# Third chunk's x loads and VectorE's order written out in a block kernel's ramp, and one gate product moved by a slot

## The chip, the cores and the metric

The kernel runs on one core of a Trainium2 chip. A core has TensorE (PE, with its weight loads shown apart as PEld), VectorE (DVE), ScalarE (ACT), GpSimd (POOL) and SyncE (SP, which here only issues DMAs); each works through its own list of instructions in order and waits on semaphores of the others. The metric is the device time of one execution in microseconds, lower is better; the time before is the median of three runs.

## The reference

The input is x of 2048 rows by 640. A layer norm (without scale or shift) gives xn. The output is the sum of x, a windowed attention on xn and a gated MLP on xn:

```python
x = A_x
xn = _layernorm(x, axis=-1)
return x + _A_ref(xn, A_wqkv, A_wo) + _B_ref(xn, B_w_gate, B_w_up, B_w_down)
```

The attention has 32 heads of 20 columns; query i sees keys i-255 to i. The MLP is `(gelu(xn @ w_gate) * (xn @ w_up)) @ w_down` with 1728 hidden columns and the tanh form of gelu. Everything is float32.

## The kernel before, in words

Float32 precision is kept by splitting each operand into a high part (rounded to the matmul's type) and a low remainder and adding three products: high*high, low*high, high*low. So each product of 640 rows of weights is 15 matmuls (5 blocks of 128 rows, 3 products). Names ending in h and l, `xh` and `xl` above all, are the two parts.

**The ramp.** The 2048 rows of x are four chunks of 512, each four tiles `xi` of 128 rows. For a chunk, VectorE takes the statistics of each tile (`ln_stats`: two BN_STATS and one BN_AGGR, lines 149 to 151), works out the reciprocal root (`ln_sqrt`, `ln_rstd`, lines 156 to 165) and scales the tile (`ln_apply`, line 169). TensorE then transposes: `turn(k, ...)` (line 185) writes the k-th block of 128 columns of all four tiles into one PSUM tile `ps_t`; k runs over five. ScalarE copies each `ps_t` to `xh` (line 193), VectorE subtracts it to give `xl` (line 194). The letter handed to `turn` says which PSUM pool the tile comes from: "x" has two buffers, "m" four. In `ln_turn` before, the letters alternate x m x m x, so the fifth transpose takes a buffer that the first used.

Behind each chunk's transposes stand projections of it: `proj_v` (15 matmuls into `ps_v`) for four tiles of 128 rows, one chunk behind, and `proj_qk` (15 matmuls of 512 columns into `ps_d`) for two blocks of wqk, number 0 and number 5. `save_qk` stores a `ps_d`: `upper` on ScalarE (line 277, `pt<-ps_d`), `middle` on VectorE (line 273, `r<-ps_d,pt`; `r` has a single buffer), `lower` on ScalarE (line 255), `lowest` on GpSimd (line 259), then DMAs to `qd` or `kd`.

Chunk 0 is written out by hand in `first_chunk`, under a manual schedule in which every compute engine keeps the order of the code; its last lines take the statistics of chunk 1 (tiles 4 to 7), project v for tiles 0 and 1, and scale tiles 4 to 7. The rest of the ramp is code in an ordinary loop `for c in range(1, NC)`, whose order on each engine a scheduler sets when the program is built, and it merges with the end of the manual part too. The x tiles have eight buffers, so tiles 8 to 11 take those of 0 to 3, and their loads wait for the transposes of these; SyncE issues all DMAs of this stage in one order.

**The attention.** 32 units (8 groups of 4 heads, 4 chunks) run as a stream of 14 slots each (`NS = 14`), the order of every engine as written. In slots 0, 5 and 9 `pull_max(2, T)` emits two pairs of score products (`ps_m`, line 508) and VectorE's row maxima of them (line 518; two to a pair, in four PSUM buffers). In slot 0 a second `pull_max(2, T)` follows the product with v (`av_unit`, `ps_o`, line 616). Odd slots below 12 have two score products for the exponentials (`ps_e`, line 573) and ScalarE's exponentials (line 575). Between these, `pull_fill` feeds dense matmuls as filling: projections, and later the first gate and up products of the MLP (`gate_up_fill`).

A function that must come later is given to `defer(n, fn)`, which runs it n slots on; one wrapped in `late` runs at the slot's `flush()`, in slot 0 behind the first `pull_max` and the `av_unit`. A gate's chain is c1 (ScalarE: half of the product and its square, lines 670 and 671), c2 (VectorE: the product `he<-he,gs`, line 676), c3 (ScalarE: tanh, line 680; `lag()` slots after c2, one from slot 13, three from slot 0), c4 and c5 (VectorE, lines 684 and 691). There are 12 such gates.

**After the attention** come the rest of the MLP and the output product, both also written out; the change does not touch them.

Of the kernel before, what the change touches and what calls it, by code (L numbers as in the profile page):

```python
# [9 lines left out]
F32 = mybir.dt.float32  # L10
# [10 lines left out]
NC = S // C  # L21
# [9 lines left out]
NS = 14  # L31
# [36 lines left out]
def block_kernel(ctx, tc, x, wqk, wv, wgu, wdo, wdl, out):  # L68
# [73 lines left out]
    def ln_load(t, lp):  # L142
        xi = lp.tile([128, D], F32, name="xi", tag="xi", bufs=8)
        nc.sync.dma_start(xi, x[t * 128:(t + 1) * 128, :])
        return xi

    def ln_stats(xi, mv, lp):
        st = lp.tile([128, 2, 6], F32, name="st", tag="st", bufs=4)
        nc.vector.bn_stats(st[:, 0, :], xi[:, 0:320])  # L149
        nc.vector.bn_stats(st[:, 1, :], xi[:, 320:640])  # L150
        nc.vector.bn_aggr(mv, st)
# [16 lines left out]
    def ln_apply(xi, mv, rs):  # L168
        nc.vector.tensor_scalar(xi, xi, mv[:, 0:1], rs, op0=OP.subtract, op1=OP.mult)

    def ln_scale(xs, lp):
        n = len(xs)
        mv = lp.tile([128, n, 2], F32, name="mv4", tag="mv4", bufs=2)
        for i, xi in enumerate(xs):
            ln_stats(xi, mv[:, i, :], lp)
        rs = ln_rstd(*ln_sqrt(mv, n, lp), n, lp)
        for i, xi in enumerate(xs):
            ln_apply(xi, mv[:, i, :], rs[:, i:i + 1])

    def turn(k, xs, where):  # L180
        n = len(xs)
        pool, tag = {"x": (psx, "ex"), "m": (psm, "mx"), "o": (psm, "mx")}[where]
        ps = pool.tile([128, n * 128], F32, name="ps_t", tag=tag)
        for i in range(n):
            nc.tensor.transpose(ps[:, i * 128:(i + 1) * 128], xs[i][:, k * 128:(k + 1) * 128], ident)  # L185
        return ps

    def ln_turn(t0, xs):
        n = len(xs)
        cs = slice(t0 * 128, (t0 + n) * 128)  # L190
        for k in range(KT):
            ps = turn(k, xs, "xm"[k % 2])
            nc.scalar.activation(xh[:, k, cs], ps, AF.Copy)
            nc.vector.tensor_tensor(out=xl[:, k, cs], in0=ps, in1=xh[:, k, cs].bitcast(F32), op=OP.subtract)  # L194

# [23 lines left out]
    def defer(n, fn, *a):  # L219
        if now[0] is None:  # L220
            fn(*a)
        else:
            at(now[0] + n, fn, *a)
# [121 lines left out]
    def first_chunk(xs, wr0, wr5, prep, v0, lp):  # L345
# [26 lines left out]
        with tc.manual_schedule(engines=MANUAL | {mybir.EngineType.Pool}):  # L372
# [27 lines left out]
            for k in range(KT):  # L400
                low(k, ta[k], halves[0])
            tb = [turn(k, xs[2:4], "oxmxm"[k]) for k in range(KT)]
            for k in range(KT):
                high(k, tb[k], halves[1])
            for k in range(KT):
# [20 lines left out]
            for j in range(4):  # L426
                ln_apply(xs[4 + j], mv[:, j, :], rs[:, j:j + 1])
            save_qk(0, 0, dn[0])
            save_qk(5, 0, dn[1])
        return w0, w5, v0  # L430

    v0 = []
    with tc.tile_pool(name="lp", bufs=1, side="right") as lp:
        xs = [ln_load(t, lp) for t in range(2)]
        wr0 = load_qk(0)
        xs += [ln_load(t, lp) for t in (2, 3)]
        wr5 = load_qk(5)
        warm = lp.tile([128, 256], BF, name="warm")[:, 0:128]
        nc.vector.memset(warm, 0.0)
        ps = psd.tile([128, C], F32, name="ps_u", tag="dn")  # L440
        for i, n in enumerate(WARM):
            if i:
                nc.tensor.transpose(ps[:, 0:128], xs[1][:, 0:128], ident)
            for _ in range(n):
                nc.tensor.matmul(ps[:, 0:128], warm, warm, start=True, stop=True)
        prep = load_v(0, v0, lp, v_tiles())
        next(prep)
        xs += [ln_load(t, lp) for t in range(4, 8)]
        w0, w5, v0 = first_chunk(xs, wr0, wr5, prep, v0, lp)
        ones = lp.tile([4, 2 * C], BF, name="ones")  # L450
        nc.gpsimd.memset(ones, 0.0)
        nc.gpsimd.memset(ones[0:2], 1.0)
        for i in range(NK):
            for j in (0, 2):
                nc.sync.dma_start(ks[i][SR:64, j:j + 2].rearrange("p j t -> p (j t)"), ones)
        for c in range(1, NC):
            if c > 1:
                ln_scale(xs[4 * c:4 * c + 4], lp)
            ln_turn(4 * c, xs[4 * c:4 * c + 4])
            if c + 1 < NC:  # L460
                xs += [ln_load(t, lp) for t in range(4 * c + 4, 4 * c + 8)]
            if c == 1:
                for i in range(NQ):
                    for j in (0, 2):
                        nc.sync.dma_start(qs[i][SR + 2:64, j:j + 2].rearrange("p j t -> p (j t)"), ones[2:4])
            if c == 2:
                raws1 = [load_qk(1), load_qk(6)]
            if c < NC - 1:
                run(*[proj_v(v0, 4 * c - 4 + i, None if i % 2 else (psm, "mx")) for i in range(0 if c > 1 else 2, 4)])
                run(proj_qk(0, w0, c), proj_qk(5, w5, c))  # L470
# [191 lines left out]
    def gate_up_fill(f, ws, c):  # L662
# [4 lines left out]
        def c1():  # L667
            gs = st["g"] = hp.tile([128, C], F32, name="gs", tag="gs")
            t = st["t"] = hp.tile([128, C], F32, name="he", tag="he", bufs=2)
            nc.scalar.activation(gs, pss[0], AF.Copy, scale=0.5)  # L670
            nc.scalar.activation(t, pss[0], AF.Square, scale=math.sqrt(0.044715))
            defer(1, late, c2)

        def c2():
            gs, t = st["g"], st["t"]
# [853 lines left out]
```

## Time and profile before

| what | value |
|---|---|
| median of 3 runs | 1043.57 us (1043.51 to 1044.68) |
| the profiled execution | 1044.74 us, its span 1043.0 us |
| granted TensorE clock | 0.999 |
| PE busy | 1031.9 us, 99% of the span |
| DVE, ACT, POOL busy | 741.3, 528.0, 384.5 us (71%, 51%, 37%) |
| DMA moved | 158.74 MB, mean 152 GB/s |

A row of the timeline reads: start, duration (of the whole merged group), engine, line, operation, output<-input, shape, count, and in brackets the idle time of the engine just before it and what ended it. A start and the next row's start on one engine give the time that a group takes; durations of pipelined matmuls overlap. A row of the waits reads: who waited, for whom, total us, times, longest us.

### The profile page before, as it was taken

What the parts mean: (1) busy time and instruction counts of PE and PEld (TensorE: products, weight loads), DVE (VectorE), ACT (ScalarE), POOL (GpSimd) and SP (SyncE); (2) the same over time, 40 slices, a digit from 0 to 9 for tenths busy, and PEclk for the clock granted to TensorE, in tenths of its full rate; (3) what the DMA queues carried; (4) which work ended last, traced back from release to release, by engine and by line L of the source; (5) the groups of instructions that cost most, each with busy time, mean ns of one, the idle gap of its engine ahead of it and who ended that gap; (6) DMA issues with size and microseconds to landing.
All of it is one profiled execution on the core that took longest, in us unless ns stands there. A gap on an engine that the chain in (4) does not pass through costs nothing.

```text
span 1043.0 us, 25570 instructions
## 1 busy us (share of the span) xinstructions
PE 1031.9 (99%) x9396; PEld 833.9 (80%) x9396; DVE 741.3 (71%) x2018; ACT 528.0 (51%) x1120; POOL 384.5 (37%) x623
## 2 busy tenths in 40 slices
PE   8999999999999999999999999999999999999998
PEld 7987666666777666666678888888888999999998
DVE  7745666677656676677736777775556889888887
ACT  4534766767666666666675222223324554333332
POOL 5122778888765787667471111101110000000000
PEclk9999999999999999999999999999999999999999
DMA  6542356555533354343325576763117874433333
GB/s 224 181 143 70 98 168 184 160 172 160 179 94 100 116 162 147 97 130 120 97 75 192 187 244 210 247 242 120 73 62 264 255 245 135 139 127 114 124 122 107
DMA packets 102151, 158.74 MB, mean 152 GB/s; under 512 B 14173, under 2 KB 55261, under 8 KB 102025
## 3 DMA queue, kind: packets, MB, share of 16 engines
q1 hardware_dynamic: 99640, 150.94, 45.2%
q10 hardware_dynamic: 2384, 6.16, 1.9%
q8 instruction: 74, 1.21, 0.5%
q14 instruction: 53, 0.43, 0.1%
HBM read 101.78 MB, written 54.92 MB: 150 GB/s over the span
## 4 chain that ended last, share of the span: by engine, by line
PE 93%; DVE 4%; ACT 1%; DMA 1%; issue 1%; POOL 0%; DVEq 0%; SPq 0%; ACTq 0%
PE ps_g L973 23%; PE ps L1245 23%; PE ps_d L108 20%; PE ps_e L573 8%; PE ps_v L108 6%; PE ps_o L616 5%; PE ps_m L508 5%; DVE junk L518 2%; PE ps_g L108 1%; DMA xi<-x 1%; PE ps_d L356 1%; DVE xl L194 0%; PE ps_t L185 0%; DVE st L149 0%; DVE st L150 0%
## 5 line engine op out<-in xcount | busy, mean ns | idle before, releaser
L518 DVE CUSTOM_DVE_ANT_0 junk<-ps_m,mask 128x320 bf16<-128x320 f32 (+2 forms) x512 | 243.0, 475 | 129.1 <-PE ps_m L508 71.2
L575 ACT ACTIVATE P<-ps_e 128x512 f32<-128x512 f32 (+2 forms) x384 | 198.7, 572 | 68.6 <-PE ps_e L573 68.1
L1245 PE MATMUL ps<-wb,at 128*128 128x320 f32 x999 | 155.9, 309 | 0.0
L1245 PEld LDWEIGHTS ps<-wb,at 128*128 128x128 f32 x999 | 148.9, 188 | 0.2
L588 POOL TENSOR_SCALAR_AFFINE_SELECT P<-P 128x256 f32<-128x256 f32 (+1 forms) x192 | 94.1, 492 | 73.4 <-ACT P L575 70.1
L573 PE MATMUL ps_e<-qs,ks 124*128 124x128 bf16 (+2 forms) x704 | 118.3, 278 | 0.1
L108 PE MATMUL ps_d<-xl,wqh 128*128 128x512 f32 x310 | 98.5, 422 | 0.0
L108 PE MATMUL ps_d<-xh,wqh 128*128 128x512 f32 x310 | 98.2, 421 | 0.0
L108 PE MATMUL ps_d<-xh,wql 128*128 128x512 f32 x310 | 97.6, 419 | 0.0
L101 POOL TENSOR_TENSOR wql<-wr,wqh 128x640 fp32r<-128x640 f32 x12 | 19.2, 1604 | 195.7 <-PE ps_g L973 171.2
L1245 PE MATMUL ps<-wt,at 128*128 128x320 f32 x552 | 88.9, 309 | 0.0
L573 PEld LDWEIGHTS <-ks 124*128 124x128 bf16 x704 | 49.5, 98 | 48.9 <-issue 33.4
L1245 PEld LDWEIGHTS ps<-wt,at 128*128 128x128 f32 x552 | 82.9, 188 | 0.1
L591 POOL TENSOR_SCALAR_AFFINE_SELECT P<-P 128x512 f32<-128x512 f32 (+1 forms) x144 | 76.4, 539 | 16.3 <-ACT P L575 16.3
L1199 ACT ACTIVATE at<-ss 128x512 fp32r<-128x512 f32 x59 | 37.3, 632 | 84.1 <-DVE ss L1078 84.1
L616 PE MATMUL ps_o<-P,v 64*32 64x320 f32 (+4 forms) x2816 | 74.2, 347 | 0.0
L259 POOL TENSOR_TENSOR pt<-r,pt 128x512 bf16<-128x512 f32 x40 | 46.6, 1165 | 65.4 <-ACT pt L255 64.9
L616 PEld LDWEIGHTS ps_o<-P,v 64*32 64x32 f32 x2816 | 50.9, 106 | 21.5 <-issue 0.9
L508 PE MATMUL ps_m<-ks,qs 60*64 60x320 bf16 (+3 forms) x1472 | 64.5, 260 | 2.8 <-DVE mx L518 1.5
L1002 ACT ACTIVATE hr<-hr 128x512 f32<-128x512 f32 x20 | 12.6, 632 | 102.0 <-DVE hr L976 102.0
L108 PEld LDWEIGHTS ps_d<-xh,wql 128*128 128x128 f32 x310 | 56.0, 189 | 10.1 <-issue 0.9
L108 PEld LDWEIGHTS ps_d<-xh,wqh 128*128 128x128 f32 x310 | 56.0, 189 | 9.7 <-issue 1.6
(197 smaller groups left out, 1982.3 us busy)
## 6 DMA issues: line engine op xcount, KB each, us to landing
hd<-he SPq DMA_DIRECT2D x50, 256.0 KB
hr<-hd SPq DMA_DIRECT2D x48, 256.0 KB
wr<-wgu SPq DMA_DIRECT2D x27, 320.0 KB
qs<-qd SPq DMA_DIRECT2D x64, 120.0 KB
ks<-kd SPq DMA_DIRECT2D x64, 120.0 KB
xi<-x SPq DMA_DIRECT2D x16, 320.0 KB
qs<-qd SPq DMA_DIRECT2D x64, 80.0 KB
ks<-kd SPq DMA_DIRECT2D x64, 80.0 KB
```

The costliest lines, as they stand in the source:

```text
L108: nc.tensor.matmul(ps, a(k), b(k), start=n == 0, stop=n == 3 * nk - 1)
L259: nc.gpsimd.tensor_tensor(out=pt[:, l, :], in0=r, in1=pt[:, 1, :], op=OP.subtract)
L508: nc.tensor.matmul(ps[64 * h:64 * h + 64, col:col + w], q[rows, j, q0:q0 + 64], ks_, start=True, stop=True, tile_position=(64 * r, 64 * h))
L518: nc.vector.tensor_tensor_reduce(out=junk[:, 0:n], in0=ps[:, 320 - n:320], in1=mask[:, 320 - n:320], scale=1.0, scalar=NEG, op0=OP.add, op ...
L573: nc.tensor.matmul(ps[:, col:col + n], k[0:QROWS, j, kc:kc + 128], q[0:QROWS, j, q0:q0 + n], start=True, stop=True)
L575: nc.scalar.activation(pt[:, j, lo:hi], ps[:, lo:hi], AF.Exp, scale=SCALE)
L588: nc.gpsimd.affine_select(out=a, in_=a, pattern=[[0, n], [1, 128]], compare_op=OP.is_ge, fill=0.0, base=0, channel_multiplier=-1)
L591: nc.gpsimd.affine_select(out=a, in_=a, pattern=[[0, n], [-1, 128]], compare_op=OP.is_ge, fill=0.0, base=-1, channel_multiplier=1)
L616: nc.tensor.matmul(os[r][32 * j:32 * j + 32, qa:qb], v[rows, w0_:w0_ + 32], pt[rows, j, col + qa - q0:col + qb - q0], start=r not in begun ...
L973: nc.tensor.matmul(ps, i, j, start=first and n == 0, stop=n == len(work) - 1, skip_group_check=True)
L1199: nc.scalar.activation(hi[:, 3:7], s, AF.Copy)
L1245: nc.tensor.matmul(ps[bank][:, 0:HD], *work[bank][j], start=bank not in begun, stop=final[p, bank] == n and j == len(work[bank]) - 1, skip ...
```

## The change

Four edits in the ramp and one in the attention:

1. The loads of tiles 8 to 11 move from the loop's first round into `first_chunk`, right behind the transposes of tiles 2 and 3 in the code. The loop no longer loads in its first round.
2. The statistics of tiles 8 and 9 are taken inside the manual part, between `save_qk(0, 0, ...)` and its end; their tile `mv` is handed out and `ln_scale` for chunk 2 begins at tile 10.
3. `save_qk(5, 0, ...)` stands outside the manual part.
4. The transposes of chunks 1 and 2 take PSUM buffers "xmxmm" in place of "xmxmx"; chunk 3 keeps "xmxmx".
5. A gate whose c1 falls in slot 12 defers c2 by two slots, to slot 0 of the next unit, and not by one to slot 13.

```diff
-    def ln_scale(xs, lp):
+    def ln_scale(xs, lp, mv=None, begun=0):
         n = len(xs)
-        mv = lp.tile([128, n, 2], F32, name="mv4", tag="mv4", bufs=2)
-        for i, xi in enumerate(xs):
-            ln_stats(xi, mv[:, i, :], lp)
+        mv = mv or lp.tile([128, n, 2], F32, name="mv4", tag="mv4", bufs=2)
+        for i in range(begun, n):
+            ln_stats(xs[i], mv[:, i, :], lp)
...
-    def ln_turn(t0, xs):
+    def ln_turn(t0, xs, where="xmxmx"):
...
-            ps = turn(k, xs, "xm"[k % 2])
+            ps = turn(k, xs, where[k])
...
             tb = [turn(k, xs[2:4], "oxmxm"[k]) for k in range(KT)]
+            xs += [ln_load(t, lp) for t in range(8, 12)]
...
             save_qk(0, 0, dn[0])
-            save_qk(5, 0, dn[1])
-        return w0, w5, v0
+            mv = lp.tile([128, 4, 2], F32, name="mv4", tag="mv4", bufs=2)
+            for j in range(2):
+                ln_stats(xs[8 + j], mv[:, j, :], lp)
+        save_qk(5, 0, dn[1])
+        return w0, w5, v0, mv
...
             if c > 1:
-                ln_scale(xs[4 * c:4 * c + 4], lp)
-            ln_turn(4 * c, xs[4 * c:4 * c + 4])
-            if c + 1 < NC:
+                ln_scale(xs[4 * c:4 * c + 4], lp, *((mv, 2) if c == 2 else ()))
+            ln_turn(4 * c, xs[4 * c:4 * c + 4], "xmxmx" if c == NC - 1 else "xmxmm")
+            if 1 < c < NC - 1:
                 xs += [ln_load(t, lp) for t in range(4 * c + 4, 4 * c + 8)]
...
-            defer(1, late, c2)
+            defer(2 if now[0] is not None and now[0] % NS == NS - 2 else 1, late, c2)
```

What this does to the engines' orders is seen in four places. The first is VectorE between the statistics of tile 7 and the scaling of chunk 1. Before (`mv_470` is chunk 1's statistics, `mv_705` chunk 2's):

```order
L156 TENSOR_TENSOR ve<-mv_470,one 128x4
L162 RECIPROCAL rs<-sq 128x4
L151 BN_AGGR mv_705<-st 128x2
L149 BN_STATS st<-xi 128x6
L163 TENSOR_TENSOR ve<-ve,rs 128x4
L150 BN_STATS st<-xi 128x6
L164 SCALAR_TENSOR_TENSOR ve<-ve,rs 128x4
L149 BN_STATS st<-xi 128x6
L165 SCALAR_TENSOR_TENSOR rs<-ve,rs 128x4
L151 BN_AGGR mv_705<-st 128x2
L150 BN_STATS st<-xi 128x6
L169 TENSOR_SCALAR xi<-xi,mv_470,rs 128x640 x4
```

The same place on VectorE after the change (`mv_478` is chunk 1's statistics, `mv_556` chunk 2's):

```order
L156 TENSOR_TENSOR ve<-mv_478,one 128x4
L162 RECIPROCAL rs<-sq 128x4
L163 TENSOR_TENSOR ve<-ve,rs 128x4
L164 SCALAR_TENSOR_TENSOR ve<-ve,rs 128x4
L165 SCALAR_TENSOR_TENSOR rs<-ve,rs 128x4
L169 TENSOR_SCALAR xi<-xi,mv_478,rs 128x640 x4
L273 TENSOR_TENSOR r<-ps_d,pt 128x512
L149 BN_STATS st<-xi 128x6
L150 BN_STATS st<-xi 128x6
L194 TENSOR_TENSOR xl_81<-ps_t,xh_77 128x512
```

The statistics of tiles 8 to 10, which stood in front of chunk 1's scaling, stand behind it.

The second place is VectorE around the scaling of chunk 2. Before (`mv_910` is chunk 3's statistics):

```order
L156 TENSOR_TENSOR ve<-mv_705,one 128x4
L151 BN_AGGR mv_910<-st 128x2
L162 RECIPROCAL rs<-sq 128x4
L163 TENSOR_TENSOR ve<-ve,rs 128x4
L164 SCALAR_TENSOR_TENSOR ve<-ve,rs 128x4
L165 SCALAR_TENSOR_TENSOR rs<-ve,rs 128x4
L169 TENSOR_SCALAR xi<-xi,mv_705,rs 128x640 x4
L273 TENSOR_TENSOR r<-ps_d,pt 128x512
```

And after; the two L273 are `middle` for wqk blocks 0 and 5 of chunk 1:

```order
L163 TENSOR_TENSOR ve<-ve,rs 128x4
L150 BN_STATS st<-xi 128x6
L273 TENSOR_TENSOR r<-ps_d,pt 128x512
L164 SCALAR_TENSOR_TENSOR ve<-ve,rs 128x4
L151 BN_AGGR mv_910<-st 128x2
L149 BN_STATS st<-xi 128x6
L165 SCALAR_TENSOR_TENSOR rs<-ve,rs 128x4
L150 BN_STATS st<-xi 128x6
L169 TENSOR_SCALAR xi<-xi,mv_556,rs 128x640 x3
L273 TENSOR_TENSOR r<-ps_d,pt 128x512
L169 TENSOR_SCALAR xi<-xi,mv_556,rs 128x640
```

Statistics of tiles 13 and 14 and both `middle` steps have come in front of the scaling of chunk 2's last tile; before, the four scalings stood together and in front of both.

The third place is TensorE at the transposes of chunk 2. Before:

```order
L108 MATMUL ps_d<-xl_81,wqh 128x512 x5
L185 MATMUL ps_t<-ident,xi 128x128 x16
L108 MATMUL ps_v<-wvh,xh_77 128x320 x3
L185 MATMUL ps_t<-ident,xi 128x128 x4
L108 MATMUL ps_v<-wvh,xh_77 128x320 x2
```

And after:

```order
L108 MATMUL ps_d<-xl_81,wqh 128x512 x5
L185 MATMUL ps_t<-ident,xi 128x128 x15
L108 MATMUL ps_v<-wvh,xh_77 128x320 x2
L185 MATMUL ps_t<-ident,xi 128x128 x5
L108 MATMUL ps_v<-wvh,xh_77 128x320 x3
```

The 16 went block by block over all four tiles, and the 4 were the fifth block; the 15 are the blocks of tiles 8, 9 and 10, tile by tile, and the 5 are tile 11. In chunk 1 the 16 and 4 become 20 together.

The fourth place is VectorE at the first of the three gates that the fifth edit moves, where a unit begins; the ISA rows are maxima and the reads of their result. Before:

```order
L518 ISA mx 128x1
L676 SCALAR_TENSOR_TENSOR he<-he,gs 128x512
L518 ISA junk,mx<-ps_m,mask 128x320
L518 ISA mx 128x1
L518 ISA junk,mx<-ps_m,mask 128x320
```

And after (lines below the edits in the ramp carry numbers four higher):

```order
L522 ISA junk,mx<-ps_m,mask 128x320
L522 ISA mx 128x1
L522 ISA junk,mx<-ps_m,mask 128x320
L522 ISA mx 128x1
L680 SCALAR_TENSOR_TENSOR he<-he,gs 128x512
L522 ISA junk,mx<-ps_m,mask 128x320
```

The product has moved behind the four maxima of slot 0's first pull. On ScalarE the gate's tanh moves with it, from in front of the two copies of `ps_o` to behind the next two exponentials. SyncE issues the loads of tiles 8 and 9 right behind those of tiles 4 to 7, tiles 10 and 11 behind three of the eight small loads of ones that `ks` needs, tile 13 between the stores of `qd` and `kd`, and the second of the two loads of `wr` behind tile 15.

More of the change, by code (lines that the diff above doesn't have):

```diff
@@ L448, in block_kernel @@
         xs += [ln_load(t, lp) for t in range(4, 8)]
[L449 removed]
+        w0, w5, v0, mv = first_chunk(xs, wr0, wr5, prep, v0, lp)
         ones = lp.tile([4, 2 * C], BF, name="ones")
```

## The prediction

> **What bounds the kernel.** I read the page first, then TensorE's waits, then the timeline where they fall.
>
> ```profile
> span 1043.0 us, 25570 instructions
> PE 1031.9 (99%) x9396; PEld 833.9 (80%) x9396; DVE 741.3 (71%) x2018; ACT 528.0 (51%) x1120; POOL 384.5 (37%) x623
> ```
>
> TensorE is the bound: whatever it stands still less, the kernel should be shorter by. It has only these waits for other engines in the whole span:
>
> ```profile
> PE ps_t L185 <- DVE xi L169: 2.5, 4, 1.1
> PE ps_m L508 <- DVE mx L518: 1.5, 5, 0.4
> PE ps_t L185 <- DVE xl L194: 0.8, 2, 0.6
> ```
>
> All name VectorE: transposes that wait for scaled x tiles, score products that wait for maxima to free PSUM, and a fifth transpose that waits for `xl` to free its buffer. The change works at all three. TensorE in the ramp (gap before the group in brackets):
>
> ```profile
> 23.48 0.90 PE L108 MATMUL ps_v<-wvl,xh 128*128 128x320 f32 x5
> ...
> 25.42 2.46 PE L185 MATMUL ps_t<-ident,xi 128*128 128x128 f32 x16 [1.05 <-DVE xi L169]
> ...
> 30.36 0.90 PE L108 MATMUL ps_v<-wvh,xh 128*128 128x320 f32 x5
> ...
> 32.56 1.32 PE L108 MATMUL ps_d<-xh,wqh 128*128 128x512 f32 x5
> ...
> 39.39 1.91 PE L185 MATMUL ps_t<-ident,xi 128*128 128x128 f32 x16
> 41.05 0.69 PE L108 MATMUL ps_v<-wvh,xh 128*128 128x320 f32 x3
> 42.38 0.66 PE L185 MATMUL ps_t<-ident,xi 128*128 128x128 f32 x4 [0.65 <-DVE xl L194]
> 42.80 0.54 PE L108 MATMUL ps_v<-wvh,xh 128*128 128x320 f32 x2
> ```
>
> The group at 25.42 is chunk 1's transposes, late by 1.05 us; that at 39.39 is chunk 2's, not late, but its fifth block waits 0.65 at 42.38. VectorE over the same stretch shows why:
>
> ```profile
> 19.36 0.48 DVE L150 BATCH_NORM_STATS2 st<-xi 128x6 f32<-128x320 f32 x1
> 20.54 0.49 DVE L149 BATCH_NORM_STATS2 st<-xi 128x6 f32<-128x320 f32 x1 [0.70 <-DMA xi<-x]
> ...
> 23.73 0.49 DVE L149 BATCH_NORM_STATS2 st<-xi 128x6 f32<-128x320 f32 x1 [0.99 <-DMA xi<-x]
> ...
> 27.23 0.67 DVE L273 TENSOR_TENSOR r<-ps_d,pt 128x512 f32<-128x512 f32 x1
> ...
> 30.75 1.96 DVE L194 TENSOR_TENSOR xl<-ps_t,xh 128x512 fp32r<-128x512 f32 x3
> 32.62 0.48 DVE L150 BATCH_NORM_STATS2 st<-xi 128x6 f32<-128x320 f32 x1
> ...
> 34.87 2.18 DVE L169 TENSOR_SCALAR xi<-xi,mv,rs 128x640 f32<-128x640 f32 x4
> ```
>
> Chunk 1's statistics end with the row at 19.36. Then VectorE waits twice for loads of tiles 8 and 10, which chunk 1 has no need of, with chunk 1's scaling queued behind.
>
> **Chunk 1's transposes (edits 1 to 4).** The statistics of tiles 8 to 10 leave the way. By the rows at 32.62 and 34.87, 2.25 us lie between a late statistics row and the scaling, and that stretch holds another tile's statistics as well. So chunk 1's scaling starts by 19.36 + 2.25 = 21.6 and, at 2.18 for four, ends by 23.8. TensorE is ready when v of tile 1 is issued: a group of five v matmuls takes (32.56 - 30.36)/3 = 0.73, so at 23.48 + 0.73 = 24.21. It no longer waits. Sixteen transposes without a wait took 41.05 - 39.39 = 1.66, 0.104 each; twenty take 2.08, to 26.29. All five fit without a wait for `xl`, since "m" has a buffer free for the fifth. Two v tiles (2 x 2.20) reach 30.69, two wqk blocks (39.39 - 32.56 = 6.83) reach 37.52. TensorE comes to chunk 2's transposes 39.39 - 37.52 = 1.87 us earlier.
>
> **Chunk 2's transposes: what is late next.** VectorE's work has not gone, it stands later. Its order from the end of chunk 1 on, started by ScalarE's copy:
>
> ```profile
> 24.89 0.63 ACT L277 ACTIVATE pt<-ps_d 128x512 bf16<-128x512 f32 x1
> 27.26 1.09 ACT L193 ACTIVATE xh<-ps_t 128x512 fp32r<-128x512 f32 x2 [1.74 <-PE ps_t L185]
> ...
> 39.63 0.60 ACT L277 ACTIVATE pt<-ps_d 128x512 bf16<-128x512 f32 x1 [1.31 <-POOL pt L259]
> ```
>
> ```profile
> 28.94 1.17 POOL L259 TENSOR_TENSOR pt<-r,pt 128x512 bf16<-128x512 f32 x1 [9.28 <-ACT pt L255]
> ```
>
> `pt` is ready at 25.52. I price a statistics row at 0.40 (two in a row before), a `r` at 0.67, an `xl` at (32.62 - 30.75)/3 = 0.62, an aggregation between others at 0.12. From 25.6: r 26.3, tile 8 27.1, one xl and its aggregation 27.8, tile 9 28.6, r and aggregation 29.4, four xl 31.9. ScalarE's copies (0.55 each) and GpSimd's step (1.17) run ahead of these and do not hold them. Then: tile 10 and half of tile 11 1.3 (33.2), the stretch like 32.62 to 34.87 2.25 (35.45), and in between, new here, the four rows of tiles 13 and 14, r and an aggregation, 1.6 + 0.67 + 0.12 = 2.4. The first scaling starts at 37.8, or at 37.3 if the small steps hide between the larger ones as they may. TensorE is ready at 37.52, and needs a scaled tile some 0.75 after a scaling starts. So these transposes now wait for VectorE.
>
> There is more. GpSimd's step of 1.17 us for the `r` in this stretch starts 0.67 + 0.63 + 0.15 = 1.45 after that r, the scaling about 1.7 after it (r, aggregation, two statistics rows and the small steps). They overlap, GpSimd 0.25 ahead. Once in the trace a scaling met a GpSimd operation:
>
> ```profile
> 10.95 0.94 POOL L452 MEMSET ones<- 2x1024 bf16 x1
> ...
> 11.36 0.88 DVE L169 TENSOR_SCALAR xi<-xi,mv,rs 128x640 f32<-128x640 f32 x1
> ```
>
> The scaling took 0.88 in place of 0.61, and ended 0.35 behind the memset's end at 11.89. I take it that it was held till then. The Trainium skill ("SBUF — State Buffer", section "Who interferes with whom") says that VectorE's tensor_scalar in a 2-port mode and GpSimd share one port pair, locked for a whole instruction by whichever starts first; the row agrees. With the hold, GpSimd ends at 38.2 to 38.7, the first scaling at 38.55 to 39.05, the third (0.545 each) at 39.65 to 40.15. Then the second r stands in front of the fourth scaling; its `pt` is there (TensorE 37.52 + 0.24 + 0.60 = 38.4, by the rows at 39.39 and 39.63). The fourth ends 0.61 + 0.55 later, at 40.8 to 41.3, and tile 11's five transposes are over 0.14 + 0.52 later: 41.45 to 41.95. Before, the same work (20 transposes, two v matmuls) was over at 42.80 - 0.15 = 42.65. The ramp gains 0.7 to 1.2; without the hold 1.3 to 1.85; with VectorE no limit at all, 2.75. I take 1.1, near the upper end of the case with the hold, as small steps hid well before.
>
> Hidden and priced at nothing: the earlier x loads wait on SyncE for transposes of tiles 0 to 3, but the loads of ones behind them wait for GpSimd's memset to 11.89 anyway, and ones, like `wr`, is used only after the ramp. If that cover went, SyncE's later loads would slip (rival 4). Behind chunk 2's transposes stand four v tiles, 8.8 us, over which VectorE finishes `xl`. Chunk 3's order is as before.
>
> **The gate's product (edit 5).** Three of twelve are moved. The first, on TensorE and VectorE, and the other two on TensorE:
>
> ```profile
> 428.85 0.72 DVE L676 SCALAR_TENSOR_TENSOR he<-he,gs 128x512 f32<-128x512 f32 x1 [1.27 <-ACT he L671]
> 429.50 0.48 DVE L518 CUSTOM_DVE_ANT_0 junk<-ps_m,mask 128x320 bf16<-128x320 f32 x1
> ```
>
> ```profile
> 431.25 0.46 PE L508 MATMUL ps_m<-ks,qs 60*64 60x320 bf16 x5
> ...
> 432.23 0.73 PE L108 MATMUL ps_d<-xh,wql 128*128 128x512 f32 x2
> ...
> 444.98 0.33 PE L508 MATMUL ps_m<-ks,qs 60*64 60x320 bf16 x4
> ...
> 446.44 0.73 PE L108 MATMUL ps_d<-xh,wql 128*128 128x512 f32 x2
> ...
> 460.40 0.46 PE L508 MATMUL ps_m<-ks,qs 60*64 60x320 bf16 x5
> ...
> 461.35 0.73 PE L108 MATMUL ps_d<-xh,wql 128*128 128x512 f32 x2
> ```
>
> The product waits for ScalarE and takes 0.65 of VectorE ahead of the first maximum. The second pull's eight score products then need 0.98, 1.46 and 0.95 us. Another unit has its product already behind the four maxima:
>
> ```profile
> 402.76 0.91 DVE L676 SCALAR_TENSOR_TENSOR he<-he,gs 128x512 f32<-128x512 f32 x1
> ...
> 402.81 0.47 PE L508 MATMUL ps_m<-ks,qs 60*64 60x320 bf16 x8
> 403.21 0.73 PE L108 MATMUL ps_d<-xh,wqh 128*128 128x512 f32 x2
> ```
>
> There the eight need 0.40, and VectorE's product starts at 402.76 without holding anybody. So the first and third lose 0.58 and 0.55. The second loses 1.06, but gets back no more than the 0.65 by which its maxima come earlier; I take 0.6. The sum is 1.75 by starts; the waits named by the profile give less, since part of the gap lies under the modelled ends. The tanh, now behind two exponentials, finds ScalarE idle; VectorE's second four maxima start as before.
>
> **Sum.** 1.1 + 1.75 = 2.85 us of the profiled span of 1043.0 (its run took 1044.74, 1.2 over the median). From the median 1043.57 that leaves 1040.7, 0.27% less. About 0.2%, 2.1 us, is what a measurement of this kernel can tell from no change.
>
> **Rivals.**
> 1. No hold by GpSimd: GpSimd ends first or the scaling starts first, by a margin of 0.25 us. Ramp 1.3 to 2.0, together 3.05 to 3.75, 1039.8 to 1040.5. For it: a lead so small. Against: the row at 11.36.
> 2. VectorE is later still in chunk 2, from one wait of 0.7 more. Ramp 0.4, together 2.1, 1041.4. For it: VectorE, not TensorE, sets this stretch, so each delay counts in full.
> 3. The moved product only hands its wait to the second four maxima. Ramp alone, 1042.5. Against: the unit at 402.76.
> 4. Slower: the loads of tiles 13 and 14 come too late. Their statistics stand in VectorE's order ahead of chunk 2's scaling.
>
> ```profile
> 33.68 1.40 SPq L144 DMA_DIRECT2D xi<-x  x3
> ```
>
> ```profile
> 38.27 0.49 DVE L149 BATCH_NORM_STATS2 st<-xi 128x6 f32<-128x320 f32 x1 [0.61 <-DMA xi<-x]
> ```
>
> Before, tile 13 took 4.6 us from issue to statistics. After, tile 14 is issued behind the stores of the second r, at about 32.4 (29.3 + 0.6 + 1.3 for ScalarE and GpSimd, 1.2 for stores), so it is there by 37.0. It is needed at 36.3 to 36.9, and up to 0.7 of lateness vanishes under GpSimd's hold. Beyond, each us costs one; for 0.2% slower, 1045.7, it would have to land 5 us later, at about 42.
> 5. The ramp's gain and the gates' are given back later, no change. Against: 99% busy, and the orders behind are the same.
>
> **Chances.** Forecast 0.42; rival 1 0.20; rival 2 0.18, half of it past 0.2%; rival 3 0.10; rival 4 0.03; rival 5 0.07. Faster by over 0.2%: 0.42 + 0.20 + 0.09 = 0.71; within: 0.26; slower: 0.03. The range takes in the forecast and rivals 1 and 2 (0.80) with 0.2 to 0.5 us of scatter: 1039.6 to 1042.0.
>
> **What would show it.** Right: no wait at chunk 1's 20 transposes, which start near 24.2; chunk 2's start near 38.5 and wait for scaled tiles, with one scaling longer than 0.61 beside GpSimd; eight score products in 0.40 at the first and third moved gate. Wrong: a wait of VectorE for x loads between 30 and 37, transposes of tile 11 over after 42.6, or a wait for maxima still there at the gates.

## The result and the profile after

The changed kernel takes 1042.3 us, the median of 22 executions (1041.73 to 1044.85). The kernel before, run beside it, takes 1044.71 us (22 executions, 1043.51 to 1046.68). The ratio is 0.9975, with a 95% interval of 0.9969 to 0.9982: 1.9 to 3.2 us less, 2.6 in the middle. The profiled execution took 1043.06 us, its span is 1041.3 us, 1.7 less than the span of the profile before.

TensorE's waits for other engines in the changed kernel (total us, times, longest us):

```profile
PE ps_t L185 <- DVE xi L169: 1.2, 3, 0.8
PE ps_u L449 <- DVE warm L443: 1.2, 1, 1.2
PE ps_m L512 <- DMA qs<-qd: 1.1, 2, 0.6
PE ps_m L512 <- DVE mx L522: 0.6, 2, 0.4
PE ps_t L185 <- DVE xl L194: 0.2, 1, 0.2
PE ps_m L512 <- DVE xl L194: 0.2, 1, 0.2
```

The three waits that the change works at went from 2.5, 1.5 and 0.8 us to 1.2, 0.6 and 0.2. The third row is new: score products wait for a load of `qs`. The second and the last row stand in the profile before as well, with the same 1.2 and 0.2 us.

**The ramp.** The timeline of the changed kernel on TensorE, VectorE and GpSimd:

```profile
24.18 2.34 PE L185 MATMUL ps_t<-ident,xi 128*128 128x128 f32 x20
...
38.56 2.03 PE L185 MATMUL ps_t<-ident,xi 128*128 128x128 f32 x15 [0.82 <-DVE xi L169]
...
40.73 0.77 PE L185 MATMUL ps_t<-ident,xi 128*128 128x128 f32 x5
...
49.84 1.32 PE L108 MATMUL ps_d<-xh,wqh 128*128 128x512 f32 x5
```

```profile
21.29 2.18 DVE L169 TENSOR_SCALAR xi<-xi,mv,rs 128x640 f32<-128x640 f32 x4
...
37.19 2.37 DVE L169 TENSOR_SCALAR xi<-xi,mv,rs 128x640 f32<-128x640 f32 x3
39.48 0.68 DVE L273 TENSOR_TENSOR r<-ps_d,pt 128x512 f32<-128x512 f32 x1
40.08 0.60 DVE L169 TENSOR_SCALAR xi<-xi,mv,rs 128x640 f32<-128x640 f32 x1
```

```profile
37.00 1.16 POOL L259 TENSOR_TENSOR pt<-r,pt 128x512 bf16<-128x512 f32 x1 [5.54 <-ACT pt L255]
```

And the row in the profile before that answers to TensorE's last:

```profile
51.24 1.32 PE L108 MATMUL ps_d<-xh,wqh 128*128 128x512 f32 x5
```

Chunk 1's twenty transposes come without a wait. Chunk 2's wait 0.82 us for scaled tiles, and three scalings take 2.37 us beside GpSimd's step. At the projection of chunk 2, TensorE is 51.24 - 49.84 = 1.40 us ahead. I call this difference, of one matmul's start in the profile before and of the same matmul's start in another profile, the lead.

**The gates.** Score products on TensorE after, around the first moved gate, and the same two groups before:

```profile
428.75 0.47 PE L512 MATMUL ps_m<-ks,qs 60*64 60x256 bf16 x16
431.53 0.47 PE L512 MATMUL ps_m<-ks,qs 60*64 60x320 bf16 x8
435.36 0.47 PE L512 MATMUL ps_m<-ks,qs 60*64 60x256 bf16 x16
```

```profile
428.47 0.47 PE L508 MATMUL ps_m<-ks,qs 60*64 60x256 bf16 x16
...
431.25 0.46 PE L508 MATMUL ps_m<-ks,qs 60*64 60x320 bf16 x5
431.97 0.33 PE L508 MATMUL ps_m<-ks,qs 60*64 60x320 bf16 x3 [0.26 <-DVE mx L518]
...
435.67 0.47 PE L508 MATMUL ps_m<-ks,qs 60*64 60x256 bf16 x16
```

From one group of sixteen to the next it took 435.67 - 428.47 = 7.20 us and takes 6.61: 0.59 gained, and the eight in between stand together, where five and three stood apart before. At the second and third gate the lead grows by 0.60 and 0.57 us, over all three by 1.76.

**What is given back.** The lead is not 1.40 us when the gates come but -0.28 (428.47 against 428.75). Most of it goes here. `qs` holds a unit's queries, loaded back from `qd` by six DMAs, and `wr` raw weights; SPq rows are SyncE's issues. TensorE and SyncE after:

```profile
166.32 0.27 PE L512 MATMUL ps_m<-ks,qs 60*64 60x256 bf16 x1 [0.60 <-DMA qs<-qd]
167.10 0.47 PE L512 MATMUL ps_m<-ks,qs 60*64 60x256 bf16 x15 [0.51 <-DMA qs<-qd]
```

```profile
157.91 0.86 SPq L234 DMA_DIRECT2D wr<-wqk  x2
158.88 1.32 SPq L268 DMA_DIRECT2D qd<-pt  x2
160.30 4.74 SPq L487 DMA_DIRECT2D qs<-qd  x6
```

Before, the same sixteen score products start at 166.70, and the view names no wait:

```profile
166.70 0.65 PE L508 MATMUL ps_m<-ks,qs 60*64 60x256 bf16 x16
```

The landing records of the trace, where each of these DMAs lands in sixteen parts or eleven, show why TensorE waited (start of the issue, when the last but one of the parts was there, when the last):

```
load      issued   last but one   last part
wr  (1st) 157.91   160.78         160.79
wr  (2nd) 158.35   162.28         164.71
qs  (2nd) 160.84   163.88         166.19
qs  (5th) 162.36   165.28         166.96
qs  (6th) 164.72   167.23         167.55
```

Of the second `wr` load one part in sixteen landed 2.43 us behind the others, and in each of the seven DMAs behind it, too, one part came 1.7 to 2.4 us late. Two of the seven are the second and the fifth load of `qs`, and it is their semaphores that TensorE waits for here: it goes on at 166.32, 0.13 us behind the last part of the second, and at 167.10, 0.14 behind that of the fifth. The Trainium skill ("DMA: Bandwidth & Descriptors", section "Why a DMA increments its semaphore by 16 and not by 1") says that only the full count means that all data has landed; the rows agree, one late part holds the whole DMA.

SyncE was held as well. It issues a DMA only when the one eight before it is there, and the sixth load of `qs` is eighth behind that `wr` load, so it was not issued before 164.72. But these score products do not wait for the sixth load: they went on at 167.10, and it was there at 167.55.

### The profile page after: what moved, and what is told of

It reads as the page before. It is cut to its first block, busy times and chain, and to the rows that moved or that the text cites. A ratio compares the mean times of both kernels' runs of the same rounds, so it can differ in the third digit from the quotient of the medians.

```text
span 1041.3 us, 25568 instructions
## 1 busy us (share of the span) xinstructions
PE 1031.8 (99%) x9396; PEld 834.4 (80%) x9396; DVE 740.3 (71%) x2018; ACT 527.9 (51%) x1120; POOL 384.5 (37%) x623
## 4 chain that ended last, share of the span: by engine, by line
PE 92%; DVE 5%; DMA 1%; issue 1%; ACT 1%; SPq 0%; DVEq 0%; ACTq 0%
PE ps_g L977 24%; PE ps L1249 23%; PE ps_d L108 19%; PE ps_e L577 8%; PE ps_v L108 6%; PE ps_o L620 5%; PE ps_m L512 5%; DVE junk L522 2%; PE ps_g L108 1%; PE ps_d L356 1%; DVE xi L169 0%; DMA qs<-qd 0%; PE ps_t L185 0%; DVE st L150 0%; DVE xl L194 0%
## 5 line engine op out<-in xcount | busy, mean ns | idle before, releaser
L1203 ACT ACTIVATE at<-ss 128x512 fp32r<-128x512 f32 x59 | 37.3, 632 | 83.3 <-DVE ss L1082 83.3
```

Source lines behind the costliest of these rows:

```text
L1203: nc.scalar.activation(hi[:, 3:7], s, AF.Copy)
```

## The experiments

Two theories stood at the beginning: A, the ramp's gain is given back since TensorE runs into loads that do not come earlier with it; B, that was chance in one execution. From the fifth run on a third, D: the profile before showed a ramp that was worse than most. Where a lead is given, it is against the first profile before. "At 57 us" is behind the ramp, "at 300 us" behind the stretch with the late loads and ahead of the gates.

### The changed kernel again, and its parts alone

No edit in the first; in the second the gate's edit taken back; in the third it alone, on the kernel before:

```diff
-            defer(2 if now[0] is not None and now[0] % NS == NS - 2 else 1, late, c2)
+            defer(1, late, c2)
```

> The changed kernel once more. Its first profiled execution gained 1.40 us in the ramp and 1.68 us at the three gates, but lost 1.25 us at 166 us, where score products waited 0.60 and 0.51 us for a load of qs, and 0.36 us around 155 us. Theory A (the loads of this stretch set the pace: the ramp's gain brings TensorE to 166 us before the load that it needs, in most executions): a wait for qs at 166 us again, of 0.2 to 1.3 us, and a span of 1040.2 to 1041.4 us. Theory B (the wait was chance in that one execution): no wait for qs, TensorE 1.0 us or more ahead of the kernel before at 170 us, and a span near 1040.0 us.

> The four edits in the ramp without the gate's. Both theories: TensorE 1.40 us ahead of the kernel before at 57 to 151 us, and the waits for maxima at the three gates as before (1.68 us by starts). Theory A: the loads near 160 us take 0.3 to 1.3 us of it back, so that 0.1 to 1.1 us is left, 0.5 us in the median. Theory B: 1.4 us is left at the end. Rival C (the ramp's edits are worth nothing and all comes from the gates): no change.

> The kernel before with the gate's edit alone. The edit lies far behind the stretch at 150 to 170 us, so by both theories its gain of 1.68 us (0.50, 0.63 and 0.55 at the three gates) stays to the end: 1.5 to 1.8 us less than before, and the ramp as before. Rival C (the gates give back what they gain in the dense stage behind them): less than 0.5 us.

The changed kernel again: 1042.71 us, ratio 0.9982 (0.9973 to 0.9991). No wait is named at 166 us this time, but one at 238 us:

```profile
237.05 0.21 PE L512 MATMUL ps_m<-ks,qs 60*64 60x64 bf16 x1
238.23 0.36 PE L512 MATMUL ps_m<-ks,qs 60*64 60x64 bf16 x11 [0.97 <-DVE r L273]
```

VectorE's `r`, which the row names, was over at 237.89. The fifth `qs` load of that unit, issued at 232.91, had all of its parts but one by 235.66 and the last at 238.14, and the products start 0.09 us later. So the place changes, and again it is one late part; neither theory had it so.

The ramp alone: 1044.06 us, ratio 1.0 (0.9991 to 1.0009), although its profile kept a lead of 1.44 us at 57 us and 1.46 us at the end. The gate alone: 1042.08 us, ratio 0.9983 (0.9974 to 0.9992), the lead growing by 1.75 us at the three gates and staying. So by these medians nearly all of the change's worth was its fifth edit, as rival C of the ramp's run had it.

### The second wr load behind the qs loads

In the changed kernel, for one pair of blocks:

```diff
-                    raws = [load_qk(after[1]), load_qk(after[1] + 5)] if ...
+                    raws = [load_qk(after[1] + 5 * n) for n in range(1 if i == 2 else 2)] if ...
...
                     yield from proj_qk(i, ws[0], c)
+                    if i == 2 and c == 1:
+                        raws.append(load_qk(after[1] + 5))
```

> The changed kernel with one DMA moved: the second of the two 320 KB loads of wr that SyncE issues at 158 us goes behind the six loads of qs and the two stores of kd. Theory A in its narrow form (SyncE issues a DMA only when the one eight before it has landed, and the sixth load of qs stood eight behind that wr): SyncE no longer stands still 2.0 us ahead of the sixth load, no wait for qs at 166 us, TensorE 1.0 to 1.2 us ahead of the kernel before at 170 us, and 0.5 to 1.0 us less than the changed kernel in the median. Theory B: the same time as the changed kernel, within 0.3 us.

The profile was as theory A has it: sixteen score products at 165.74 without a wait, lead 1.13 us at 170 us, and 2.99 us at the end. The median was not better: 1042.32 us, ratio 0.9982 (0.9973 to 0.9991). SyncE stood still all the same, 1.9 us in the issue of the fourth load, and the last parts came at most 1.3 us behind the others in this stretch. Since the sixth load, which the edit sets free, was not the one that TensorE had waited for, this profile cannot be put down to the edit, and the median does not tell A from B.

### The kernel before again, and the early loads alone

The ramp alone having been worth nothing, the profile before was in question. The first run has no edit; the second is edit 1 by itself:

```diff
             tb = [turn(k, xs[2:4], "oxmxm"[k]) for k in range(KT)]
+            xs += [ln_load(t, lp) for t in range(8, 12)]
...
-            if c + 1 < NC:
+            if 1 < c < NC - 1:
```

> The kernel before, a second profiled execution. The four edits of the ramp alone took nothing off the median (ratio 1.0, 0.9991 to 1.0009), although TensorE was 1.44 us ahead at 57 us in their profile. Theory D (the profiled execution of the kernel before had loads of tiles 8, 10 and 13 that landed later than they do in most executions, so the ramp had less to gain than its profile showed): a wait of chunk 1's transposes well under 1.05 us, down to none, and a span shorter than 1043.0 us by as much as the ramp is. Theory A (the ramp's loss is in all executions, and the load stretch at 150 to 240 us takes the gain back): 1.05 and 0.3 to 0.65 us again in the ramp.

> The kernel before with the first edit alone: SyncE issues the loads of tiles 8 to 11 some 10 us earlier, and no other engine's order changes. VectorE's two waits for them (0.70 and 0.99 us) should go, and chunk 1's scaling comes 1.69 us earlier, at 23.0 us, so that its transposes start at 24.2 to 24.3 us without a wait. Theory A: 0.8 to 1.7 us ahead at 57 us, and 0 to 0.8 us less in the median after what the loads take back. Theory D: the same profile, but no change of the median (within 0.3 us), since most executions had no such wait.

The second profile before, VectorE and TensorE:

```profile
20.36 0.49 DVE L149 BATCH_NORM_STATS2 st<-xi 128x6 f32<-128x320 f32 x1 [0.44 <-DMA xi<-x]
...
22.73 0.49 DVE L149 BATCH_NORM_STATS2 st<-xi 128x6 f32<-128x320 f32 x1 [0.18 <-DMA xi<-x]
```

```profile
24.43 2.46 PE L185 MATMUL ps_t<-ident,xi 128*128 128x128 f32 x16
...
41.73 0.66 PE L185 MATMUL ps_t<-ident,xi 128*128 128x128 f32 x4 [0.98 <-DVE xl L194]
```

The waits for tiles 8 and 10 are 0.44 and 0.18 us here, not 0.70 and 0.99: in the first profile the last part of tile 10 came at 23.70, 1.19 us behind the last but one, in this one 0.26 us behind. Chunk 1's transposes wait so little that the row names no wait. A part of it comes back as 0.98 in place of 0.65 at chunk 2's fifth block, since VectorE waits for tile 13, whose last part was 1.53 us late. The lead of this ramp at 57 us is 0.66 us, with no edit at all. So theory D holds in part: the ramp still loses, but less.

The early loads alone had a lead of 1.72 us at 57 us, more than all four edits together, and chunk 2's transposes came at 37.60 without a wait. Only the fifth block was held:

```profile
37.60 1.91 PE L185 MATMUL ps_t<-ident,xi 128*128 128x128 f32 x16
39.27 0.69 PE L108 MATMUL ps_v<-wvh,xh 128*128 128x320 f32 x3
40.68 0.65 PE L185 MATMUL ps_t<-ident,xi 128*128 128x128 f32 x4 [0.73 <-DVE xl L194]
```

In the median 1043.63 us, ratio 0.9997 (0.9988 to 1.0005): no difference that can be told. Eight of its eleven executions took 1043.0 to 1044.1 us, three 1045.3 to 1046.3.

### The gate with the moved load, and parts measured twice

The edits are those above, on the kernel before (first and third) and the ramp's four (second).

> The kernel before with the gate's edit and with the second wr load moved, the ramp as before. TensorE does not come early to the load stretch here, so by both theories the moved load is worth nothing: the time of the gate's edit alone, 1.7 to 2.0 us less than before (ratio 0.998). If it is 0.5 us or more better than that edit alone, the load stretch holds up the kernel before as well. The ramp of its profile is one more sample for theory D.

> The four edits of the ramp alone, measured a second time. So far: TensorE was 1.3 to 1.44 us ahead of the first profile of before at 57 us in the five profiles with all four edits; before's own further ramps were 0.21, 0.42 and 0.66 us ahead of it, so the typical gain at 57 us is some 1.0 us. Between 150 and 245 us the kernels with a shorter ramp lost 0.13 to 1.66 us, those without lost 0.15 at most. Theory A+D (both): 0.2 to 0.5 us left in the median. Rival (all kept): 1.0 us. Rival (all lost): 0.0 us.

> The gate's edit alone, measured a second time beside the ramp's edits: 1.7 to 2.0 us less than before by all theories, and within 0.5 us of the changed kernel.

Gate with moved load: 1042.47 us, ratio 0.9979 (0.9970 to 0.9988); the gate alone again 1042.28 us, 0.9983 (0.9974 to 0.9992). So the moved load is worth nothing that shows where TensorE does not come early. The ramp alone again: 1044.1 us, 0.9994 (0.9985 to 1.0003). Its profile has the prediction's rival 4, VectorE and TensorE:

```profile
37.33 0.49 DVE L149 BATCH_NORM_STATS2 st<-xi 128x6 f32<-128x320 f32 x1 [1.02 <-DMA xi<-x]
...
38.38 1.64 DVE L169 TENSOR_SCALAR xi<-xi,mv,rs 128x640 f32<-128x640 f32 x3
```

```profile
39.02 2.03 PE L185 MATMUL ps_t<-ident,xi 128*128 128x128 f32 x15 [1.42 <-DVE xi L169]
```

Tile 14 was issued at 32.26 and there at 37.31. VectorE waits 1.02 us for it, and the lead at 57 us is 0.94, not 1.40 us. The scalings, now behind GpSimd's step (over at 38.03), take 1.64 us.

### GpSimd's step held behind the scaling

In the changed kernel, first with a copy that GpSimd's own order then put behind the step, and again with a copy into the place that the step writes:

```diff
-            behind(lowest)
+            if (t, c) == (0, 1):
+                held.append((pt[:, l, 0:1], lowest))
+            else:
+                behind(lowest)
...
                 ln_scale(xs[4 * c:4 * c + 4], lp, *((mv, 2) if c == 2 else ()))
+            if c == 2:
+                first, lowest = held.pop()
+                nc.gpsimd.tensor_copy(first, xs[10][:, 0:1])
+                lowest()
```

> The changed kernel with GpSimd's step on r of chunk 1 made to wait for the scaling of tile 10 (a 1-column copy of that tile ahead of it); nothing else moves. In the changed kernel the three scalings took 2.37 us beside that step, against 0.61 + 2 x 0.545 = 1.70 alone. Hold theory (the scaling is held until GpSimd's step ends): the three take 1.7 us, chunk 2's transposes start 0.6 to 0.7 us earlier, at 37.9 us, and TensorE is 2.0 us ahead of the kernel before at 57 us. Without a hold (the long scaling has another reason): 2.37 us again and no gain. In the median 0 to 0.65 us less than the changed kernel, by what the load stretch takes back.

> The changed kernel with GpSimd's step on r of chunk 1 made to wait for the scaling of tile 10 (GpSimd first copies one column of that tile into the place that the step then writes). The earlier try left the step where it was: GpSimd's order had the copy behind it. The order now also has the four scalings together, ahead of the second r, and chunk 2's twenty transposes together. Hold theory: four scalings take 2.2 us without a stretch, from 37.0 us on; the twenty transposes start at 37.8 to 38.1 us, follow the scalings and are over by 40.2 us (41.25 in the changed kernel); TensorE is 2.2 to 2.5 us ahead of the first profile of before at 57 us. Without a hold: the first scaling still takes 0.97 + 0.31 us or so, and the lead at 57 us is 1.4 to 1.9 us. In the median 0 to 1.0 us less than the changed kernel, by what late loads take back.

The first run changed nothing that it was made for: the step ran at 37.10 as before, and three scalings took 2.12 us; 1042.29 us, ratio 0.9979 (0.9970 to 0.9988). The second did it:

```profile
37.67 2.17 DVE L169 TENSOR_SCALAR xi<-xi,mv,rs 128x640 f32<-128x640 f32 x4
```

```profile
39.44 0.45 POOL L469 CAST pt<-xi 128x1 bf16<-128x1 f32 x1 [7.85 <-DVE xi L169]
39.96 1.17 POOL L263 TENSOR_TENSOR pt<-r,pt 128x512 bf16<-128x512 f32 x1
```

```profile
38.33 2.66 PE L185 MATMUL ps_t<-ident,xi 128*128 128x128 f32 x20 [0.43 <-DVE xi L169]
```

Four scalings take 2.17 us, as in the kernel before, without a stretch. They start at 37.67 and not at 37.0, in part since VectorE again waited for a tile's load (0.21). So the twenty transposes start at 38.33, 0.2 to 0.5 us later than expected, and the lead at 57 us is 1.62 us. The second `r` now stands behind all four scalings, so this run differs from the changed kernel in that, too. 1041.5 us, ratio 0.9975 (0.9966 to 0.9985): no better than the changed kernel by the ratio. The stretch is gone with the overlap, but that is worth only 0.2 to 0.4 us of lead here. In one row the hold seems to work the other way round: the one-column copy, begun beside the fourth scaling, takes 0.45 us and ends 0.04 behind it, where the copy of the first try, beside no scaling, took 0.18.

### A version that beats both

Early loads, the gate's edit, and the letters for chunk 2 alone, so that VectorE keeps the order that it had before:

```diff
+            xs += [ln_load(t, lp) for t in range(8, 12)]
...
-            ln_turn(4 * c, xs[4 * c:4 * c + 4])
+            ln_turn(4 * c, xs[4 * c:4 * c + 4], {1: "xmxmx", 2: "xmxmm"}.get(c, "xmxmx"))
...
-            defer(1, late, c2)
+            defer(2 if now[0] is not None and now[0] % NS == NS - 2 else 1, late, c2)
```

The first and third run have the second `wr` load moved as well, the second has not; the fourth is the changed kernel, in the same set as the second and third.

> A version meant to beat both kernels: the first edit (early loads), the gate's edit, the letters xmxmm for chunk 2 alone, and the second wr load moved; VectorE's order in the ramp is that of the kernel before. In the profile of the first edit alone TensorE was 1.72 us ahead at 57 us, and 0.73 us of waiting was left at the fifth block of chunk 2, which the letters take away: 2.4 us ahead at 57 us. With the gates 4.1 us ahead at 470 us where no load comes late; 0.1 to 1.7 us of it is taken back at 150 to 245 us. In the median 2.4 to 3.5 us less than before (ratio 0.9967 to 0.9977); if the ramp is worth nothing at all, 1.9 us (0.9982).

> Early loads, letters xmxmm for chunk 2 and the gate's edit, with the wr loads where they were. The lead at 57 us is 2.4 us as in the version with the moved wr load. If late loads at 150 to 245 us take back what TensorE gained, this kernel loses more there than the version with the moved load: 0.3 to 1.5 us more, in the median 2.4 to 3.2 us less than before (ratio 0.9970 to 0.9977) against 3.9 us. If the moved load is worth nothing: 3.9 us less (0.9962), the same as that version within 0.5 us.

> Early loads, letters xmxmm for chunk 2, the gate's edit and the second wr load moved, measured again, since the first had five executions. Its profile was 2.45 us ahead at 57 us and lost nothing at 150 to 245 us. 3.3 to 4.3 us less than before, ratio 0.9959 to 0.9969, and faster than the changed kernel by 1.0 to 2.0 us. If the first result was luck in five executions: 2.4 us less, like the changed kernel.

> The changed kernel a third time, beside these two. By the profiles so far: 0.9 to 1.4 us ahead at 57 us, 0.1 to 1.7 us of it lost at 150 to 245 us, 1.68 us gained at the gates; 1.9 to 2.6 us less than before in the median (ratio 0.9975 to 0.9982). That the loss at 166 or 238 us is there in a third profile has a chance of one half: it was in two of six.

With the moved load: 1040.53 us and 1041.01 us (five executions each), ratios 0.9962 (0.9949 to 0.9974) and 0.9963 (0.9951 to 0.9976). Without: 1041.37 us, 0.9967 (0.9955 to 0.9980). The changed kernel beside the second and third: 1042.14 us, 0.9975 (0.9965 to 0.9985), with no wait for a late load in this profile. TensorE in the first, at chunk 2:

```profile
36.67 1.30 PE L108 MATMUL ps_d<-xl,wqh 128*128 128x512 f32 x5
37.81 2.35 PE L185 MATMUL ps_t<-ident,xi 128*128 128x128 f32 x20
39.91 0.98 PE L108 MATMUL ps_v<-wvh,xh 128*128 128x320 f32 x5
```

No wait is left at chunk 2, neither for scaled tiles nor for `xl`. The lead at 57 us is 2.45 us, and the kernel is about 1.2 us better than the changed one (0.9963 against 0.9975, of 1044.7). The two intervals overlap, but in the set that has both, all five executions with the moved load (1040.53 to 1041.61) lie below all nine of the changed kernel (1041.64 to 1043.05). Whether the moved load has a part in this can't be told, 0.4 us lying within the intervals.

These profiles speak against theory A as it was put. The loads do come earlier with TensorE: the fifth load of `qs`, issued at 164.04 in the first profile before and 162.36 in the changed kernel, was issued at 160.60, 161.13 (moved load) and 161.24 (not moved) here. None of the three lost anything at 166 us with leads of 2.4 to 2.6; the one without the moved load lost 0.5 us between 200 and 245 us.

### The leads side by side

Worked out from all profiles, by the starts of the same matmul (us; positive is earlier than in the first profile before):

```
                                  57 us   150 us   300 us   470 us    end
before, second profile             0.66    0.61     0.75     0.66    0.67
gate alone                         0.43    0.42     0.32     2.04    2.06
gate alone, again                  0.97    0.92     0.97     2.67    2.65
gate and moved load                0.22    0.19     0.39     2.09    1.35
changed                            1.40    1.38    -0.20     1.48    1.66
changed, again                     1.36    1.37    -0.26     1.40    1.39
changed, third                     1.40    1.40     1.24     2.92    3.02
ramp alone                         1.44    1.45     1.35     1.30    1.46
ramp alone, again                  0.94    0.93     0.77     0.64    0.80
changed, moved load                1.25    1.27     1.11     2.82    2.99
changed, step not held             1.30    1.30     0.89     2.57    2.70
changed, step held                 1.62    1.59     0.93     2.57    2.46
early loads alone                  1.72    1.67     1.44     1.38    1.33
early loads, letters, gate         2.67    2.62     2.17     3.87    3.63
the same with moved load           2.45    2.44     2.54     4.21    3.86
the same with moved load, again    2.61    2.58     2.80     4.44    3.93
```

Five profiles with the ramp of before (the first, at 0, among them) have a mean lead of 0.46 us at 57 us and 0.49 at 300 us. Seven with the changed ramp (all but the step held) have 1.30 and 0.70. So the ramp's edits are worth 0.84 us at 57 us on average, and 0.21 at 300 us, where single leads lie between -0.26 and 1.35. Five of all profiles (gate and moved load, step held, and the last three) lose another 0.25 to 0.76 us between 840 and 900 us; why is not shown.

## Why the prediction was right and wrong

**The time** was missed: 1040.7 us predicted, with 1039.6 to 1042.0 around it, and 1042.3 measured, 1.6 us more. Of these, 1.14 us are the step "From the median 1043.57 that leaves 1040.7". That was a median of three executions, two of which lay at the lower end: over 22 it is 1044.71, in other sets 1044.06 to 1044.72. The sign stood in the same sentence of the prediction, since the run whose profile it prices took 1044.74. The other 0.44 us are the sum: 2.85 us where the medians differ by 2.41 (2.6 by the ratio, 1.9 to 3.2), and the term that is mis-sized in it is the ramp. That the forecast of the difference lies in the interval is in part luck, since one of its two terms does not hold. The range had 0.2 to 0.5 us of scatter and nothing for a baseline that is off by 1.1.

**The gates** came out as worked: 0.58, 0.6 and 0.55 (1.73 us; the prediction writes 1.75), against 0.59, 0.60 and 0.57 in the profile and 1.8 us by the ratio of the edit alone (0.9983 twice). Taking the second gate at 0.6 and not at its whole 1.06 was right, and so was going by starts: the waits that the profile names there before (0.26, 0.58 and 0.23) add up to 1.07 us only. Rival 3, that the product only hands on its wait, did not happen.

**The ramp in the profile** went nearly step by step. Chunk 1's transposes at 24.18 (24.21 worked out), no wait, all twenty together. Chunk 2's at 38.56 (38.5), waiting for scaled tiles, with the scalings held by GpSimd. The lead was 1.40 and not 1.1 us, above the case's 0.7 to 1.2, in part since VectorE's first scaling began at 37.19, GpSimd's step was over at 38.16 and the fourth scaling at 40.67, all a little ahead of the best case (37.3, 38.2 and 40.8). TensorE's waits were misread in one place: the view has two rows more than the prediction's "only these" (`ps_u` for `warm`, 1.2 us, and `ps_m` for `xl`, 0.2 us), but both stand unchanged after, and no term rests on them.

**The hold** was the prediction's boldest step and is shown. In six profiles the first scaling ends 0.35 or 0.36 us behind the end of GpSimd's step and the third 1.38 to 1.40, wherever the first began (37.15 to 37.60); 0.35 is also what the one row had from which the prediction took it. Where the step was over first, three take 1.64 us, and where it was made to wait, four take 2.17. The Trainium skill ("SBUF — State Buffer", section "Who interferes with whom") has GpSimd and a `tensor_scalar` of VectorE in a 2-port mode contend for a shared port pair, which the first holds for its whole instruction; the runs agree. Rival 1, no hold, is out.

**What the ramp is worth** is the mis-sized term: 1.1 us in the sum. By the ratio the edits alone gave 0.0 and 0.6 us, each with 0.9 us either way, and changed kernel less gate alone gives 0.1 to 0.8; by the leads it is 0.84 us at 57 us and 0.21 at 300. Two things were left out. First, the profile before was the worst of five ramps: its waits for tiles 8 and 10 were a matter of when loads landed in that execution, and the working took them as fixed. Second, rival 5, given 0.07 with "99% busy, and the orders behind are the same": the orders are the same, the loads' landings are not, and in two of seven profiles a late one took back some 1.2 us at 166 or 238 us. There was little slack to begin with. In the first profile before, the fifth load of `qs` was there at 166.74, and of the sixteen score products all but the first follow at 166.87; in nine of all seventeen profiles they go on 0.13 or 0.14 us behind that landing, so the load, and not TensorE, sets the time there. All seven also lose 0.32 to 0.38 us at 155 us, about half of which comes back in four of them, at a 0.5 us pause of VectorE that the ramp of before does not have; what it waits for there is not shown.

**Rival 4**, late loads of tiles 13 and 14, was rated 0.03 as a way to be slower overall. As a mechanism it was in the second profile of the ramp alone, 1.02 us late, and cost 0.46 of the 1.40, the rest vanishing under the hold as the working had it (up to 0.7). The first step of rival 2, VectorE later in chunk 2 by one wait, so happened in that execution by this door. Three more profiles have such a wait of 0.12 to 0.21 us.

**Open** stays why one part of a DMA falls behind. It does in every profile, some 11 to 34 times by more than 1.5 us; most cost nothing. One suspect is on record: in 277 of all 320 such cases a 16 KB packet of the instruction queue began in the 4 us ahead of the late part, 162.50 and 235.98 us in the two that cost most; the same is so for only 31% of the other DMAs. But 172 alone of 1258 such packets have a late part within 5 us behind them, and no run here moves them, so it is not shown that they are the cause.

## What to carry to other kernels

A wait for a DMA in one profile is a sample, not a term: look at the same wait in a second profile of the same kernel before pricing its removal. Take the baseline from more than three executions, or give the range a term for its scatter. An edit that only moves an instruction between two engines in lockstep, as the gate's does, could here be priced from starts to a tenth of a us. Where work is moved earlier, the loads it will next meet must have slack; and where VectorE and GpSimd meet, order VectorE's scalings clear of GpSimd's long steps.

## What the runs showed of the hardware that was not expected

A DMA of 320 KB issued at 158.35 us had fifteen of its sixteen parts by 162.28 and the last at 164.71, and for some 4 us each DMA behind it showed the same late part. Two of these, loads of `qs` with their last parts at 166.19 and 166.96, held TensorE for 1.1 us. The first DMA also held an issue of SyncE's for 2.0 us (eight DMAs in flight), which cost nothing that the profile shows. And less of the change did more in the ramp: with the early loads, the letters for chunk 2 alone and VectorE's old order, the lead at 57 us is 2.45 to 2.67 us, against 0.94 to 1.44 with VectorE's new order.
